# Order of VectorE's spectrum products in the middle stage of an FNet + H3 kernel

## The chip, the cores and the metric

The kernel runs on one core of a Trainium2 chip. The metric is the device time of one launch in microseconds, the median over several executions. Five engines work side by side, each on its own queue in order: TensorE (matmuls; PE in the profile, PEld is its loading of weights), VectorE (DVE), ScalarE (ACT), GpSimd (POOL) and SyncE (SP), whose queue here holds DMA issues.

## What is computed

Four layers follow each other, each added to its own input, on an input of 2048 rows by 576 channels; the first two are repeated with the same weights:

```python
x = x + A(layernorm(x))   # A: Real(DFT over rows of the DFT over channels), as matmuls with given matrices
x = x + B(layernorm(x))   # B: q * (long causal convolution of kv by ssm_k, + kv * ssm_D)
x = x + A(layernorm(x))
x = x + B(layernorm(x))

kv  = shift_convolution(k, 4 taps) * v
y_f = rfft(kv, 4096 points) * rfft(ssm_k, 4096 points)     # per channel, complex product
y   = irfft(y_f)[:2048] + kv * ssm_D
B   = q * y                                                # q is the normalised x
```

The branch B's factor y depends on k, v and the filter only, not on x. The kernel makes it once, while the first layer A runs, and uses it twice. What the change touches is the complex product of the two spectra.

## The kernel before, in words

All matmuls are split for accuracy: an operand is rounded to a high part and the rest is kept as a low part, and three products (high by high, high by low, low by high) are summed in PSUM. ScalarE makes the high part and VectorE the low part (`split`, lines 97 to 99; `act_split`, lines 516 to 518).

**The main stream.** Layer A is a loop over 128 steps (4 blocks of 512 output rows, the two DFT matrices, 16 row tiles). Each step has 12 matmuls of 128x512 into the four accumulators `s` and two into `rm`, all issued by `mm` on line 75. After a block's 32 steps its result goes through the channel DFT in `hidden` (lines 276 to 289): for each of four row tiles two halves of 27 matmuls of 128x288 (operands `u` and `w`), and VectorE adds each half to the residual on line 287.

**The branch stream.** Beside it the generator `branch` makes y. Its first part ends some 200 us into the run. Its middle stage, the one that matters here, works on 64 feeds (two halves of 288 channels, 32 groups of frequencies each). A feed is a 128x576 tile loaded from a DRAM scratch `td` (line 168, in `load_after`), the signal's spectrum lines in its first 288 columns and the filter's in the others. A visit to a feed does this:

- `mid_inverse` (line 541) for an earlier feed: three matmuls, one ScalarE copy `vo`, one store to `vd`.
- `mid_kernel` (line 520): three matmuls on the filter half into a bank `pk`, then three ScalarE copies on lines 522 to 524 (all recorded on line 512). The first takes all of `pk` into `kk[:,0]`. The second copies the upper 64 partitions of that to the upper half of `kk[:,1]`. The third overwrites the upper half of `kk[:,0]` by its lower half. So `p2 = kk[:,1]` holds the imaginary part in its upper half, and `p1 = kk[:,0]` the real part twice. `p2` is complete after the second copy, `p1` after the third.
- `mid_round` (line 536): the high and low part of the previous feed's product (`yf`): one ScalarE instruction and one 128x288 instruction on line 518.
- `mid_signal` (line 527): three matmuls on the signal half into a bank `px`, then four VectorE instructions, lines 530 to 533. Line 530 is the straight product over 128 partitions, `p1 = px*p1`. Line 531 makes the lower half of `p2` as minus the upper half of `px` times the upper half of `p2`. Line 532 overwrites the upper half of `p2` by the lower half of `px` times it, and so has to follow line 531. Line 533 adds `p2` to `p1`.
- `split_feed` (line 586): high and low part (`df`) of the feed two visits on, one ScalarE instruction and one 128x576 instruction on line 518. When it has read the raw feed, the raw buffer is free and `load_feed` (line 574) can load another.

From the 38th feed on, feeds of the last part are put between (`i2_products`, lines 550 to 560): four matmuls into two banks, two ScalarE copies, two VectorE additions on line 559, two stores to `yb`. About eight visits before that the raw feeds go down from three buffers to two (lines 616 to 622).

**Banks.** `bank` (line 83) gives the PSUM banks `bk` in turn, three of them, to `pv`, `pk` and `px` of the visits, to the products of the last part and to the halves of `hidden`. A bank can be written again once its last reader is done; for `px` that is the last of lines 530, 531 and 532 in VectorE's queue.

**What sets the order.** A hand-made budget (`STEP`, `PIECE`, `I2_COST` and the numbers that `branch` yields) decides between which matmuls of the main stream a visit is written. The order of the instructions in each engine's queue is made when the program is built and isn't strictly that of the source: where an instruction has to wait for one just before it, another that was written later may stand between the two. The trace shows it. `tc.issue_after` pins an instruction behind another on its engine; `act` uses it to keep the stage's ScalarE instructions in source order. Nothing pins the four VectorE instructions of `mid_signal`.

Of the kernel before, what the change touches and what calls it, by code (L numbers as in the profile page):

```python
# [13 lines left out]
OP = mybir.AluOpType  # L14
# [8 lines left out]
HD = D // 2  # L23
# [42 lines left out]
def fnet_h3_kernel(ctx: ExitStack, tc: tile.TileContext, x, c_mat, w_re, w_im, k_pad, v, shift_k,  # L66
                   ssm_k, ssm_d, f1c, i2c, midc, out):
    nc = tc.nc
# [280 lines left out]
    def branch():  # L349
# [150 lines left out]
        def mid_half(df, o):  # L500
            ps = bank()
            mm(ps[:, :HD], mc[:, 0, :], df[0][:, o:o + HD], True, False)
            mm(ps[:, :HD], mc[:, 0, :], df[1][:, o:o + HD], False, False)
            mm(ps[:, :HD], mc[:, 1, :], df[0][:, o:o + HD], False, True)
            return ps
# [21 lines left out]
        def mid_signal(df, kk):  # L527
            px = mid_half(df, 0)
            p1, p2 = kk[:, 0, :], kk[:, 1, :]
            nc.vector.tensor_tensor(p1, px[:, :HD], p1, OP.mult)  # L530
            nc.vector.scalar_tensor_tensor(p2[lo], px[hi, :HD], -1.0, p2[hi], op0=OP.mult, op1=OP.mult)  # L531
            nc.vector.tensor_tensor(p2[hi], px[lo, :HD], p2[hi], OP.mult)  # L532
            nc.vector.tensor_tensor(p1, p1, p2, OP.add)  # L533
            return p1

# [64 lines left out]
        for i, (kind, hf, q) in enumerate(feeds):  # L600
            df = halves.pop(i)
            if kind:
                i2_products(hf, q, fcs.pop(used), df)
                load_fc(used + ahead)
                used += 1
            else:
                if len(yfs) == MID_LAG:
                    mid_inverse(*yfs.pop(0))
                    yield 0.4
                kk = mid_kernel(df)  # L610
                if product is not None:
                    yfs.append((*product[:2], mid_round(product[2])))
                yield 1.6
                product = hf, q, mid_signal(df, kk)
# [540 lines left out]
```

## Time and profile before

| | |
|---|---|
| time, median of 3 (lowest to highest) | 1190.23 us (1188.69 to 1192.36) |
| the profiled execution | 1191.32 us, its span 1189.5 us |
| clock granted to TensorE in it | 0.998 of full speed |
| middle stage, first to last product of line 530 | 219.3 to 541.3 us |

The profile shows one execution. Its page gives each engine's busy share, the span in 40 slices, and groups of instructions with mean duration and the idle time before them. Of the trace, the waits are listed by who waited for whom, the timeline has the instructions in order of time, and the chain of waits follows back what ended last. Busy time of TensorE is the union of its matmuls, whose ends are modelled and overlap; its pace is seen better from the starts.

### The profile page before, as it was taken

How to read it: one execution, taken by the hardware profiler on the slowest of the kernel's cores; microseconds unless marked ns; L12 is line 12 of the kernel's file. 1: busy time of each engine (PE TensorE's matmuls, PEld its weight loads, DVE VectorE, ACT ScalarE, POOL GpSimd, SP SyncE). 2: the span in 40 equal slices, each digit the busy share in tenths (PEclk: the TensorE clock that was granted, in tenths of full speed). 3: DMA queues.
4: the chain of work that ended last, by engine and by line, in shares of the span. 5: the costliest groups of instructions: out<-in, count | busy, mean ns of one | idle time of the engine just before them, and what ended most of it. 6: DMA issues, size and time to landing. Idle time of an engine off the chain costs nothing.

```text
span 1189.5 us, 18071 instructions
## 1 busy us (share of the span) xinstructions
PE 1168.5 (98%) x6184; PEld 987.2 (83%) x6184; DVE 872.8 (73%) x1562; ACT 650.0 (55%) x1279; POOL 75.1 (6%) x116
## 2 busy tenths in 40 slices
PE   7999999999999999999999999999999999999997
PEld 5776767888888888888888898888888888889997
DVE  7899983688777778787767665865776776775764
ACT  7865555567766668766645666534444445450200
POOL 2210000000000000001101111000000000001111
PEclk9999999999999999999999999999999999999999
DMA  9869898545656656648966777772772776795621
GB/s 340 295 197 306 269 290 267 178 139 177 225 189 198 200 160 204 186 137 239 273 197 226 235 246 231 251 250 73 255 248 71 240 273 248 266 322 158 214 83 41
DMA packets 147454, 255.65 MB, mean 215 GB/s; under 512 B 16161, under 2 KB 56353, under 8 KB 147362
## 3 DMA queue, kind: packets, MB, share of 16 engines
q1 hardware_dynamic: 111890, 210.17, 54.9%
q10 hardware_dynamic: 28560, 37.91, 9.1%
q0 software_dynamic: 6912, 6.43, 2.4%
q8 instruction: 48, 0.79, 0.3%
q14 instruction: 44, 0.36, 0.1%
HBM read 187.80 MB, written 66.65 MB: 214 GB/s over the span
## 4 chain that ended last, share of the span: by engine, by line
PE 76%; ACT 2%; DVE 2%; DMA 2%; issue 1%; POOLq 0%; ACTq 0%; DVEq 0%
PE s L75 42%; PE bk L75 29%; PE rm L75 4%; ACT flts L512 1%; ACT mid L512 1%; DMA t<-ud 1%; DVE mid L518 0%; DMA yb<-flts 0%; DMA flts<-vd 0%; DMA flts<-in_c_mat 0%; DVE flts L532 0%; DVE flts L530 0%; ACT u L98 0%; DVE flts L531 0%; DVE flts L533 0%
## 5 line engine op out<-in xcount | busy, mean ns | idle before, releaser
L75 PE MATMUL s<-mats 128*128 128x512 f32 x2088 | 543.0, 395 | 1.6 <-ACT mats L195 0.8
L75 PEld LDWEIGHTS s<-mats 128*128 128x128 f32 x2088 | 381.0, 188 | 83.2 <-issue 10.6
L99 DVE TENSOR_TENSOR mats<-flts,mats 128x512 fp32r<-128x512 f32 x206 | 141.0, 688 | 50.8 <-ACT mats L98 48.4
L98 ACT ACTIVATE mats<-flts 128x512 fp32r<-128x512 f32 x206 | 128.3, 628 | 82.6 <-PE bk L75 31.2
L75 PE MATMUL bk<-mid 128*128 128x288 f32 x704 | 127.7, 302 | 1.6 <-DVE flts L287 0.8
L75 PEld LDWEIGHTS bk<-mid 128*128 128x128 f32 x704 | 108.0, 188 | 23.7 <-ACT flts L512 5.8
L512 ACT ACTIVATE flts<-bk 128x288 f32<-128x288 f32 (+1 forms) x192 | 76.3, 406 | 90.8 <-PE bk L75 75.9
L75 PE MATMUL bk<-w,u 128*128 128x288 f32 x864 | 121.3, 296 | 1.0 <-DVE w L241 0.4
L75 PEld LDWEIGHTS bk<-w,u 128*128 128x128 f32 x864 | 117.3, 188 | 5.5 <-DVE flts L532 1.7
L518 DVE TENSOR_TENSOR mid<-flts,mid 128x576 fp32r<-128x576 f32 (+1 forms) x149 | 93.4, 629 | 18.6 <-ACT mid L512 15.2
L75 PE MATMUL rm<-mats 128*128 128x512 f32 x304 | 94.6, 391 | 0.2 <-ACT flts L512 0.2
L512 ACT ACTIVATE mid<-flts 128x576 fp32r<-128x576 f32 (+1 forms) x148 | 80.3, 575 | 11.8 <-DVE flts L533 8.5
L287 DVE TENSOR_TENSOR flts<-flts,bk 128x288 f32<-128x288 f32 x48 | 21.8, 453 | 65.8 <-PE bk L75 65.7
L451 ACT ACTIVATE flts<-bf 128x384 f32<-128x384 f32 (+1 forms) x104 | 43.2, 463 | 46.0 <-PE bf L75 45.9
L75 PE MATMUL bk<-mats 128*128 128x288 f32 (+1 forms) x376 | 67.8, 317 | 0.0
L75 PEld LDWEIGHTS rm<-mats 128*128 128x128 f32 x304 | 56.9, 188 | 12.8 <-ACT flts L512 0.6
L75 PE MATMUL s<-t,mats 128*128 128x512 f32 x264 | 65.4, 390 | 0.6 <-DVE t L99 0.3
L184 POOL TENSOR_TENSOR flts<-flts 128x1 f32<-128x1 f32 x35 | 28.7, 821 | 522.4 <-DVE flts L183 522.3
L75 PE MATMUL bk<-mats,t 128*128 128x288 f32 (+1 forms) x368 | 59.3, 303 | 0.0
L512 ACT ACTIVATE flts<-flts 64x288 f32<-64x288 f32 x128 | 56.6, 443 | 4.7
L75 PEld LDWEIGHTS s<-t,mats 128*128 128x128 f32 x264 | 49.4, 188 | 11.7 <-DVE t L99 0.8
L75 PEld LDWEIGHTS bk<-mats 128*128 128x128 f32 x376 | 55.5, 188 | 3.4
(146 smaller groups left out, 1496.7 us busy)
## 6 DMA issues: line engine op xcount, KB each, us to landing
flts<-in_c_mat SPq DMA_DIRECT2D x148, 256.0 KB, 3.3
ph<-in_c_mat SPq DMA_DIRECT2D x54, 512.0 KB, 4.5
flts<-in_c_mat SPq DMA_DIRECT2D x30, 512.0 KB, 4.8
flts<-td SPq DMA_DIRECT2D x53, 288.0 KB, 2.9
td<-flts ACTq DMA_DIRECT2D x36, 384.0 KB, 4.6
vd<-flts ACTq DMA_DIRECT2D x64, 144.0 KB, 2.7
flts<-vd SPq DMA_DIRECT2D x32, 288.0 KB, 4.1
ud<-ph ACTq DMA_DIRECT2D x12, 512.0 KB, 6.3
```

The lines of the kernel that those rows point to most:

```text
L75: return nc.tensor.matmul(ps, lhsT, rhs, start=first, stop=last, skip_group_check=more).ins
L98: a = nc.scalar.activation(h, src, AF.Copy).ins
L99: return a, nc.vector.tensor_tensor(l, src, h.bitcast(F32), OP.subtract).ins
L184: pows.append(nc.gpsimd.tensor_tensor(rs, ve, mhalf, OP.pow).ins)
L287: added[:] = [nc.vector.tensor_tensor(r[:, cs], r[:, cs], ps[:, :HD], OP.add).ins]
L451: stored[:] = [nc.scalar.activation(so[:, i, :], ps[i], AF.Copy).ins]
L512: last_act.append(nc.scalar.activation(*args, **kw).ins)
L518: nc.vector.tensor_tensor(l, src, h.bitcast(F32), OP.subtract)
```

## The change

In `mid_signal` the straight product moves from the first to the third place. The four instructions, their operands and shapes are the same.

```diff
         def mid_signal(df, kk):
             px = mid_half(df, 0)
             p1, p2 = kk[:, 0, :], kk[:, 1, :]
-            nc.vector.tensor_tensor(p1, px[:, :HD], p1, OP.mult)
             nc.vector.scalar_tensor_tensor(p2[lo], px[hi, :HD], -1.0, p2[hi], op0=OP.mult, op1=OP.mult)
             nc.vector.tensor_tensor(p2[hi], px[lo, :HD], p2[hi], OP.mult)
+            nc.vector.tensor_tensor(p1, px[:, :HD], p1, OP.mult)
             nc.vector.tensor_tensor(p1, p1, p2, OP.add)
             return p1
```

## The prediction, made before the changed kernel was seen

> **What bounds the kernel now.** I read the page first, for the engine that is never idle, then the middle stage by stretches, then TensorE's pace there.
>
> ```profile
> PE 1168.5 (98%) x6184; PEld 987.2 (83%) x6184; DVE 872.8 (73%) x1562; ACT 650.0 (55%) x1279; POOL 75.1 (6%) x116
> ...
> 245.00:325.00 80.00, 79.72 (x431) 67.99 (x430) 68.15 (x134) 61.00 (x132) 0.00 (x0) 1.00 0.58 185
> ...
> 440.00:545.00 105.00, 104.39 (x549) 88.62 (x547) 87.00 (x166) 75.89 (x162) 3.69 (x7) 1.00 0.60 178
> ```
>
> The columns of the stretches are length, then busy time of PE, PEld, DVE, ACT and POOL. TensorE is busy for 79.72 of 80 us and 104.39 of 105 us. VectorE, which the change touches, has a sixth of those stretches free. But busy matmuls overlap in the record, so I check the pace by starts in the chain of waits:
>
> ```profile
> 307.41 1.38 PE s L75 x6
> 311.80 1.38 PE s L75 x6
> ...
> 650.82 2.72 PE s L75 x12
> 654.00 2.72 PE s L75 x12
> 666.69 3.55 PE bk L75 x27
> ```
>
> Near 650 us TensorE has only the main stream. Twelve matmuls of 128x512 take 2.72 us there, 0.227 us each, and 27 of 128x288 take 3.55 us near 667 us, 0.131 us each. A regular visit of the middle stage holds 14 of the first kind and 9 of the second: 14 x 0.227 + 9 x 0.131 = 4.36 us. The visits come 311.80 - 307.41 = 4.39 us apart. So in a regular visit TensorE runs at its own pace, and whatever VectorE's order does there is worth at most 0.03 us. Only irregular places can gain, and only a new wait can lose.
>
> [...]
>
> **The change part by part.** It adds and removes nothing. What is moved is seen in one regular visit on VectorE:
>
> ```profile
> 307.27 0.69 DVE L99 TENSOR_TENSOR mats<-flts,mats 128x512 fp32r<-128x512 f32 x1 [0.70 <-ACT mats L98]
> 307.88 0.45 DVE L530 TENSOR_TENSOR flts<-bk,flts 128x288 f32<-128x288 f32 x1
> 308.25 0.45 DVE L518 TENSOR_TENSOR mid<-flts,mid 128x288 fp32r<-128x288 f32 x1
> 308.73 0.46 DVE L531 SCALAR_TENSOR_TENSOR flts<-bk,flts 64x288 f32<-64x288 f32 x1
> 309.22 0.76 DVE L518 TENSOR_TENSOR mid<-flts,mid 128x576 fp32r<-128x576 f32 x1
> 310.01 0.45 DVE L532 TENSOR_TENSOR flts<-bk,flts 64x288 f32<-64x288 f32 x1
> 310.50 0.46 DVE L533 TENSOR_TENSOR flts<-flts 128x288 f32<-128x288 f32 x1
> 311.66 0.69 DVE L99 TENSOR_TENSOR mats<-flts,mats 128x512 fp32r<-128x512 f32 x1 [0.70 <-ACT mats L98]
> ...
> 310.01 0.32 SPq L168 DMA_DIRECT2D flts<-td  x1
> ...
> 311.24 0.55 PE L75 MATMUL bk<-mid 128*128 128x288 f32 x3
> ```
>
> Line 532 depends on line 531, and the queue has the feed's split (line 518, 128x576, 0.76 us) between the two, although the source has it behind line 533. After the change the straight product is the next instruction written behind the crossed pair, it depends on neither of them, and it is written ahead of the split. So I expect it to fill that gap: 531, 530, 532, split, 533 (or 531, 532, 530, split, 533 where the small split of line 518 stands behind 531). The sum of the durations is the same, and line 533 ends where it ended. Three things move.
>
> (a) **The bank of `px` comes free earlier**, by the split that no longer stands ahead of its last reader: 310.01 - 309.22 = 0.79 us in this visit. Here it buys nothing: line 532 ends at 310.46, and the next matmuls into that bank start at 311.24. It buys something where TensorE stands waiting for that reader:
>
> ```profile
> PEld bk L75 <- ACT flts L512: 6.7, 25, 0.7
> ...
> PEld bk L75 <- DVE flts L532: 4.5, 12, 0.8
> ...
> PE bk L75 <- DVE flts L532: 0.4, 1, 0.4
> ...
> 391.06 0.86 PE L75 MATMUL s<-mats 128*128 128x512 f32 x3
> 391.97 3.58 PEld L75 LDWEIGHTS bk<-w,u 128*128 128x128 f32 x27 [0.49 <-DVE flts L532]
> ...
> 403.84 0.62 PE L75 MATMUL rm<-mats 128*128 128x512 f32 x2
> 404.33 0.45 DVE L532 TENSOR_TENSOR flts<-bk,flts 64x288 f32<-64x288 f32 x1
> 404.83 2.29 PEld L75 LDWEIGHTS bk<-w,u 128*128 128x128 f32 x17 [0.80 <-DVE flts L532]
> ```
>
> Weight loads waited 4.5 us for line 532 in 12 places; matmuls alone show 0.4 us. The loss of pace lies between. At 391.97 us three matmuls from 391.06 at 0.227 us each would have ended at 391.74, so 0.23 of the 0.49 us is lost; at 404.83 two from 403.84 would have ended at 404.29, so 0.54 of 0.80 us. Together 0.77 of 1.29, that is 60%, and 0.6 x 4.5 = 2.7 us. The longest wait is 0.80 us and the bank comes 0.79 us earlier, so I take all 2.7 us as gained. Bounds: 4.5 us gained at most, and 0 if the matmuls are also queued earlier and wait as long as before.
>
> (b) **The first product can start before the third copy of line 524**, since line 531 needs only the second:
>
> ```profile
> DVE flts L530 <- ACT flts L512: 15.2, 14, 2.2
> ...
> L512 ACT ACTIVATE flts<-flts 64x288 f32<-64x288 f32 x128 | 56.6, 443 | 4.7
> ```
>
> VectorE stood idle 14 times ahead of line 530 for ScalarE. One copy is 0.443 us, so 14 x 0.443 = 6.2 us of VectorE's idle time may go. No release to TensorE but that of (a) hangs on it, which (a) already counts in full: I take 0, with 2.7 us more as the far end of a gain, a second sum like that of (a).
>
> (c) **The feed's split comes one product later**, 0.45 to 0.49 us. Behind it on VectorE stand line 533 and the main stream's splits, which move by nothing, as the sum is equal. Behind it on SP stands the load of another feed: in the visit above it is issued at 310.01, right when the split is done, and now is issued at about 310.5. Behind that load in SP's queue stand the loads of the DFT matrix.
>
> ```profile
> SPq L168 <- DVE mid L518: 122.6, 57, 5.2
> SPq L168 <- DVE mats L99: 51.6, 39, 4.8
> ...
> 391.36 0.68 ACT L512 ACTIVATE mid<-flts 128x576 fp32r<-128x576 f32 x1 [0.62 <-DMA flts<-td]
> ...
> PEld bk L75 <- DVE mid L518: 0.7, 3, 0.3
> ```
>
> SP waits for that split in 57 places, so the lateness reaches the DMA each time. Whether it reaches TensorE is the question: the loads of the matrix wait for line 99 anyway (39 times), one feed's ScalarE half stood 0.62 us waiting for its load, and weight loads waited for the split for only 0.7 us in all. I take 0, bounded by a gain of 0 (nothing gets earlier) and the loss of the second rival.
>
> GpSimd's queue waits for nothing that moves in the steady part: its filter loads follow TensorE and the last part's buffers. Line 533 feeds `mid_round` one visit on; as its end doesn't move, neither does that.
>
> **Sum.** The profiled execution took 1191.32 us, with a span of 1189.5 us; it lies 1.1 us above the median of 1190.23 and inside the three runs. From it 2.7 us go: 1188.6 us, and from the median **1187.5 us**, -0.2%. That is less than 0.3% (3.6 us), about what a measurement of this kernel can tell from no change.
>
> **The rivals.**
>
> *Nothing reaches TensorE.* The matmuls behind the earlier bank are queued earlier too, or the planner keeps today's order with the straight product merely elsewhere. For it: the regular visit has 0.78 us to spare (310.46 to 311.24) and doesn't use it. Against: the waits at 391.97 and 404.83 us stand directly behind line 532. Time: 1190.2 us, within a microsecond.
>
> *Slower: the loop of the raw feeds.* In the later part of the stage there are two raw buffers. A buffer goes from split to SP's load, to ScalarE's half, to the split again, and the split is now a product later in each visit.
>
> ```profile
> L530 DVE TENSOR_TENSOR flts<-bk,flts x31: 447/454/459, 371.9 to 541.3; 128x288 f32<-128x288 f32 x31
> ```
>
> There are 31 visits from 371.9 us on. Passed on whole, each costs a product, 0.46 us: 31 x 0.46 = 14.3 us, 1204.5 us. It decides from 8 visits on (8 x 0.46 = 3.7 us). For it: the wait of 0.62 us at 391.36 shows a load that is only just in time. Against: only one such wait is in the list, and 0.7 us for the split on TensorE. If half of them pass it on, 7.1 us less the 2.7 gained: 1194.6 us.
>
> *Faster: ScalarE's evictions come earlier as well.* Weight loads also wait 6.7 us for ScalarE's copies out of the banks, in 25 places, 0.6 x 6.7 = 4.0 us of pace, and ScalarE itself waits for VectorE:
>
> ```profile
> ACT mid L512 <- DVE flts L533: 8.5, 9, 1.9
> ...
> ACT flts L512 <- DVE flts L531: 4.6, 10, 0.5
> ```
>
> If (b) shortens these waits, the copies behind them on ScalarE come earlier and the 4.0 us go too: 1190.2 - 2.7 - 4.0 = 1183.5 us. Against: the evictions wait mostly for TensorE. [...]
>
> **How the numbers follow.** Forecast 0.42, of which 0.06 ends beyond 3.6 us (towards all 4.5 us of (a)); nothing reaches TensorE 0.18, of which 0.02 ends beyond 3.6 us on the slow side, through other places of the queues; slower by the feeds 0.22; faster with ScalarE 0.18. So faster 0.06 + 0.18 = 0.24, slower 0.22 + 0.02 = 0.24, within 0.3% 0.36 + 0.16 = 0.52. The range reaches from 1183.5 (the faster case) to 1196.0 (the feed loop with a few visits more than half: 18 x 0.46 - 2.7 = 5.6 us), leaving out half of each outer case, some 0.2. The forecast's own range is 1185.7 to 1190.2.
>
> **What would show it.** Right: on VectorE line 530 stands between 531 and 533 ahead of the 128x576 split; the list of waits has less than 1 us of weight loads behind line 532 or 530; the visits stay 4.39 us apart. Wrong in (c): weight loads wait several us for line 518, ScalarE waits for DMAs from `td` or `vd`, and visits after 372 us are further apart. Wrong in (a): the waits for line 532 turn up behind line 530 with the same sum. If VectorE's order is otherwise than I expect, (a) and (c) both fall.

## The result, and the profile after

| | before | after |
|---|---|---|
| median of 12 runs each (lowest to highest) | 1190.38 us (1188.69 to 1195.69) | 1187.27 us (1185.74 to 1190.31) |
| the profiled execution, its span | 1191.32, 1189.5 us | 1186.46, 1184.5 us |

The ratio is 0.9972, with a 95% interval of 0.9964 to 0.9980: 3.3 us less, 2.4 to 4.3. Forecast were 2.7 us and 1187.5 us.

In the changed kernel line 530 is the first crossed product, 531 the second, 532 the straight one, now the last reader of `px`, and 533 the sum. Its page, the line of TensorE:

```profile
PE 1165.9 (98%) x6184; PEld 988.1 (83%) x6184; DVE 868.8 (73%) x1562; ACT 650.6 (55%) x1279; POOL 75.0 (6%) x116
```

The work is the same, 6184 matmuls and 1562 VectorE instructions. TensorE's busy time is 2.6 us shorter and the span 5.0 us. The difference is sought in the middle stage. First the regular visit of the prediction, on VectorE, with SP's load of a feed and the chain of waits (start, length; idle time before it in brackets):

```profile
304.46 0.69 DVE L99 TENSOR_TENSOR mats<-flts,mats 128x512 fp32r<-128x512 f32 x1 [0.70 <-ACT mats L98]
305.18 0.46 DVE L530 SCALAR_TENSOR_TENSOR flts<-bk,flts 64x288 f32<-64x288 f32 x1
305.68 0.46 DVE L518 TENSOR_TENSOR mid<-flts,mid 128x288 fp32r<-128x288 f32 x1
306.17 0.45 DVE L531 TENSOR_TENSOR flts<-bk,flts 64x288 f32<-64x288 f32 x1
306.63 0.46 DVE L532 TENSOR_TENSOR flts<-bk,flts 128x288 f32<-128x288 f32 x1
307.01 0.75 DVE L518 TENSOR_TENSOR mid<-flts,mid 128x576 fp32r<-128x576 f32 x1
307.67 0.45 DVE L533 TENSOR_TENSOR flts<-flts 128x288 f32<-128x288 f32 x1
...
307.78 0.32 SPq L168 DMA_DIRECT2D flts<-td  x1
...
304.60 1.38 PE s L75 x6
308.99 1.38 PE s L75 x6
```

The small split of line 518 stands between the crossed products, the straight product behind both, and the feed's split (128x576) behind that. The last reader ends 307.09 - 305.18 = 1.91 us after the first product starts; before it was 310.46 - 307.88 = 2.58 us. The feed's split starts 1.83 us after the first product instead of 1.34, so 0.49 us later, and SP's load 2.60 us after it instead of 2.13. The visits are still 4.39 us apart.

What has changed for TensorE shows in the waits of the stage, 215 to 545 us (who waited for whom, us in all, times, longest):

```profile
DVE flts L530 <- ACT flts L512: 10.6, 9, 2.0
...
ACT mid L512 <- DMA flts<-td: 2.2, 4, 0.7
...
PEld bk L75 <- DVE flts L532: 1.4, 4, 0.6
...
PEld bk L75 <- DVE mid L518: 0.8, 3, 0.3
...
PE bk L75 <- DVE flts L532: 0.2, 1, 0.2
```

Weight loads wait 1.4 us for the last reader, in 4 places, where it was 4.5 us in 12. They wait 0.8 us for line 518 (0.7 before). VectorE stands idle for ScalarE 10.6 us ahead of its first product instead of 15.2. The second of the two waits shown in the prediction is gone (timeline of the changed kernel, at the same matmuls):

```profile
399.21 0.46 DVE L532 TENSOR_TENSOR flts<-bk,flts 128x288 f32<-128x288 f32 x1
399.58 0.75 DVE L518 TENSOR_TENSOR mid<-flts,mid 128x576 fp32r<-128x576 f32 x1
...
400.77 0.62 PE L75 MATMUL rm<-mats 128*128 128x512 f32 x2
401.01 3.74 PEld L75 LDWEIGHTS bk<-w,u 128*128 128x128 f32 x27
401.24 3.75 PE L75 MATMUL bk<-w,u 128*128 128x288 f32 x27
```

The two matmuls into `rm` start at 400.77, at 0.227 us each they end at 401.22, and the next matmul starts at 401.24. Before, 0.54 us were lost here.

Where the time went can be counted over all matmuls. Taking from each distance between two starts TensorE's own pace (0.227 or 0.131 us) and summing what is left from 212 to 560 us gives 16.2 us lost before and 13.0 us after. At the matmuls whose load waits for the last reader of `px` it is 3.1 us before (12 places) and 0.9 us after (4). This counts the held matmul and the one behind it, which mostly starts another 0.11 us late, as at 404.83 and 405.07 us before; the held ones alone make 1.8 and 0.5 us. The same matmuls of the main stream start 1.2 us earlier already ahead of the stage (209.1 and 207.9 us), where both kernels have the same code, and 4.8 us earlier behind it (at 590 us). So in this pair of profiled executions 3.6 us lie between these two points, and 1.2 us are a difference between executions. Of the 3.6 us some 2.2 are seen directly behind the last reader; the rest is spread over other places.

### The profile page after: what moved, and what is told of

It is laid out like the page before. It is cut to its first block, busy times and chain, and to the rows that moved or that the text cites. A ratio compares the mean times of both kernels' runs of the same rounds, so it can differ in the third digit from the quotient of the medians.

```text
span 1184.5 us, 18056 instructions
## 1 busy us (share of the span) xinstructions
PE 1165.9 (98%) x6184; PEld 988.1 (83%) x6184; DVE 868.8 (73%) x1562; ACT 650.6 (55%) x1279; POOL 75.0 (6%) x116
## 4 chain that ended last, share of the span: by engine, by line
PE 77%; ACT 2%; DMA 1%; DVE 1%; issue 0%; ACTq 0%; POOLq 0%; DVEq 0%
PE s L75 43%; PE bk L75 30%; PE rm L75 4%; ACT flts L512 1%; ACT mid L512 1%; DMA t<-ud 1%; DMA flts<-in_c_mat 0%; ACT mats L98 0%; DVE mid L518 0%; DVE flts L532 0%; DVE flts L531 0%; DVE t L99 0%; ACT u L98 0%; POOLq L1151 0%; ACTq L548 0%
## 5 line engine op out<-in xcount | busy, mean ns | idle before, releaser
L75 PEld LDWEIGHTS s<-mats 128*128 128x128 f32 x2088 | 381.0, 188 | 82.2 <-issue 10.6
```

What stands on the lines that cost most here:

```text
L75: return nc.tensor.matmul(ps, lhsT, rhs, start=first, stop=last, skip_group_check=more).ins
```

## The experiments

Four causes were possible: the bank of `px` is free earlier (part (a)); the first product starts before the third copy (b); the split comes later (c, a cost); and a fourth that the prediction hadn't priced. When VectorE's order changes, the order of TensorE's queue is made anew too: 477 of the 6184 matmuls stand at another place, all between the 1045th and the 2889th. The runs with "old tensor" in their name pin the matmuls to the order that they have in the kernel before, by an order without a wait (`NoSync`) between each matmul and the next (`mm` appends every matmul to `traced`; the pieces are cut out of the source):

```python
traced = []
...
queue = [traced[a + i] for a, n in ORDER_OF_MATMULS for i in range(n)]
for one, two_ in zip(queue, queue[1:]):
    tc.add_manual_dep(two_, one.name, mybir.DependencyInfo(
        mybir.DependencyClass.NoSync, mybir.DependencyReason.DATA), reason="order of matmuls")
```

In the pinned kernels the lines stand further down: `mm` on 101 or 102, ScalarE on 539 or 540, the split on 545 or 546, the products from 557 to 563. The table has all runs. "Gained" is (1 - ratio) x 1191 us with the interval worked out in the same way. "Reader" and "split" are weight loads' waits for the last reader of `px` and for line 518 (in before, after, e1, e7 and e8 all of these places but one are behind a 128x576 split, in e10 all), "first" is VectorE's wait for ScalarE ahead of its first product, all in us between 215 and 545 us.

| kernel | split in between | early start | TensorE's queue | ratio (95%) | gained, us | reader | split | first |
|---|---|---|---|---|---|---|---|---|
| before | 54 | no | old | 1 | 0 | 4.5 | 0.7 | 15.2 |
| after | 18 | yes | new | 0.9972 (0.9964 to 0.9980) | 3.3 (2.4 to 4.3) | 1.4 | 0.8 | 10.6 |
| e1 | 0 | no | made anew | 0.9994 (0.9985 to 1.0003) | 0.7 (-0.4 to 1.8) | 1.2 | 1.8 | 16.9 |
| e7 | 0 | no | old | 0.9988 (0.9979 to 0.9996) | 1.4 (0.5 to 2.5) | 0.6 | 2.6 | 13.8 |
| e3 | 48 | yes | made anew | 0.9984 (0.9975 to 0.9993) | 1.9 (0.8 to 3.0) | 1.4 | 0.6 | 11.4 |
| e9 | 48 | yes | old | 0.9994 (0.9986 to 1.0003) | 0.7 (-0.4 to 1.7) | 2.4 | 1.1 | 9.7 |
| e4 | 20 | no | made anew | 0.9989 (0.9980 to 0.9998) | 1.3 (0.2 to 2.4) | 2.1 | 1.0 | 17.5 |
| e8 | 21 | no | old | 0.9999 (0.9990 to 1.0007) | 0.1 (-0.8 to 1.2) | 1.6 | 1.6 | 16.2 |
| e5 | 19 | yes | old | 0.9978 (0.9969 to 0.9987) | 2.6 (1.5 to 3.7) | 0.9 | 0.5 | 10.2 |
| e6 | 52 | no | of after | 1.0033 (1.0021 to 1.0044) | -3.9 (-5.2 to -2.5) | 3.6 | 0.5 | 15.5 |
| e10 | 0 | yes | old | 0.9968 (0.9956 to 0.9980) | 3.8 (2.4 to 5.2) | none | 0.7 | 10.2 |
| e12 | 0 | yes | made anew | 0.9958 (0.9944 to 0.9972) | 5.0 (3.3 to 6.7) | 0.6 | 0.9 | 9.8 |
| e2 | 0 | yes | made anew | 0.9992 (0.9983 to 1.0001) | 1.0 (-0.1 to 2.0) | 2.0 | 0.9 | 10.2 |
| e11 | 0 | yes | old | 0.9988 (0.9979 to 0.9997) | 1.4 (0.4 to 2.5) | 0.5 | 0.5 | 12.3 |

"Split in between" counts, of 64 visits, those in which a 128x576 split stands between the first product and the last reader of `px`; where it doesn't, the bank is early. From the first product's start to the last reader's end it takes 2.43 us on the mean before, 2.04 after, 1.86 in e1, 2.41 in e9 and 1.84 in e12.

A second measure can be read from each trace: the time between the starts of the 1041st and the 2901st matmul, between which all moved ones lie. Against before it is shorter by 3.4 us in after, 3.3 in e12, 3.1 in e10, 2.6 in e5, 2.3 in e3, 1.5 in e1, 1.4 in e4, 1.3 in e9, 0.7 in e11, 0.3 in e2 and e8 and 0.2 in e7, and longer by 2.5 us in e6. Each is one execution, but the order is nearly that of the times.

### The bank alone: e1_source_order_split_behind

The source order of before, and the feed's split pinned behind the last reader of `px` (`behind` puts `tc.issue_after` around what it encloses; `kind` is 0 for a feed of this stage):

```diff
-            nc.vector.tensor_tensor(p2[hi], px[lo, :HD], p2[hi], OP.mult)
+            last_px[:] = [nc.vector.tensor_tensor(p2[hi], px[lo, :HD], p2[hi], OP.mult).ins]
...
-            split_feed(i + 2)
+            with behind(*(last_px if not kind else [])):
+                split_feed(i + 2)
```

> The source order of before (straight product first), with one thing pinned: the 128x576 split of line 518 stands behind the last product that reads the bank of px, in all 64 visits (before: ahead of it in most). The first product still waits for the third copy. Theory A, the bank that comes free earlier: 2.5 to 4.5 us under before, as fast as the changed kernel or a little faster, and weight loads wait under 1.5 us for the last product. Theory B, the earlier start of the first product: within 1 us of before. Theory C, another draw of queue order without a mechanism: anywhere within 4 us of before, and the waits for the last product don't go along with the time.

0.9994 (0.9985 to 1.0003). The waits of e1 in the stage:

```profile
ACT mid L512 <- DMA flts<-vd: 3.3, 3, 1.3
ACT mid L512 <- DMA flts<-td: 2.9, 4, 1.1
PEld bk L75 <- DVE mid L518: 1.8, 6, 0.4
...
PEld bk L75 <- DVE flts L532: 1.2, 5, 0.4
```

The wait for the last reader went from 4.5 to 1.2 us, as part (a) says, but the time hardly followed: weight loads now wait 1.8 us for the split, and ScalarE 6.2 us for transfers of feeds (0.6 before). Part (a) alone, with (b) and (c) taken as 0, doesn't carry the result.

### The straight product in the middle: e2_straight_in_the_middle

```diff
-            nc.vector.tensor_tensor(p1, px[:, :HD], p1, OP.mult)
             nc.vector.scalar_tensor_tensor(p2[lo], px[hi, :HD], -1.0, p2[hi], op0=OP.mult, op1=OP.mult)
+            nc.vector.tensor_tensor(p1, px[:, :HD], p1, OP.mult)
             nc.vector.tensor_tensor(p2[hi], px[lo, :HD], p2[hi], OP.mult)
```

> Straight product in the second place, between the crossed ones; nothing pinned. In VectorE's queue the 128x576 split then stands behind the last reader of px in all visits but 2, in the changed kernel in 44 of 64. Theory A: at least the gain of the changed kernel, 3 to 4.5 us under before. Theory B: the first product still starts without the third copy, so the same gain as the changed kernel, 3 us. Theory C: no better guess than within 4 us of before.

0.9992 (0.9983 to 1.0001), although it has the early bank and the early start. Between the crossed products stands now the straight one, often with the small split of line 518, and in no visit the feed's split. I come back to it at e11.

### The split kept ahead: e3_split_ahead

The changed order, with the straight product pinned behind the feed's split, so that the bank comes free as late as before; `split_feed` is called from `mid_signal`, directly behind `mid_half`, and returns its VectorE instruction:

```diff
-        def mid_signal(df, kk):
+        def mid_signal(df, kk, i):
             px = mid_half(df, 0)
+            low = split_feed(i)
...
-            nc.vector.tensor_tensor(p1, px[:, :HD], p1, OP.mult)
+            with behind(*low):
+                nc.vector.tensor_tensor(p1, px[:, :HD], p1, OP.mult)
```

> The changed order, with the feed's split written ahead of the products and the straight product (the last reader of px) pinned behind it: the bank comes free as late as in before or later, the start of the first product stays early. Theory A: the gain is lost, at before or up to 3 us slower, and weight loads wait 4 us or more behind line of the straight product. Theory B: the gain stays, 2 to 4 us under before. Theory C: within 4 us of before either way.

0.9984 (0.9975 to 0.9993): the early start without the early bank, and a gain of 1.9 us, though with a queue of TensorE of its own.

### The start taken away: e4_first_waits_for_third_copy

The changed order, whose first crossed product waits for the third copy as the straight product did:

```diff
+            copy3[:] = [last_act[-1]]
...
-            nc.vector.scalar_tensor_tensor(p2[lo], px[hi, :HD], -1.0, p2[hi], op0=OP.mult, op1=OP.mult)
+            first = nc.vector.scalar_tensor_tensor(p2[lo], px[hi, :HD], -1.0, p2[hi], op0=OP.mult, op1=OP.mult).ins
+            tc.add_manual_dep(first, copy3[0].name, mybir.DependencyInfo(
+                mybir.DependencyClass.Sync, mybir.DependencyReason.DATA), reason="third copy")
```

> The changed order, with one wait more: the first crossed product waits for the third ScalarE copy, as the straight product did in before. The order of the queue is nearly that of the changed kernel (split behind the last reader of px in 42 visits instead of 44). Theory A: as the changed kernel, 2 to 4 us under before. Theory B: the gain is lost, within 1 us of before. Theory C: within 4 us of before either way.

0.9989 (0.9980 to 0.9998). It lies between what was expected for the bank and for the start. These four kernels each got a queue of TensorE of their own, and their gains, 0.7 to 1.9 us, don't order the causes. So the next runs hold that queue still.

### VectorE's order or TensorE's: e5_new_vector_old_tensor and e6_old_vector_new_tensor

e5 is the changed source with the matmuls in the order of before. e6 is the source of before with the matmuls in the order of after.

> The changed source, with all matmuls pinned in TensorE's queue to the order that they have in before. The first four runs took theory A down as it stood (source order with the split behind: 1 us, not 3), so it is now: D, the gain lies in the order of TensorE's queue, which the build makes anew when VectorE's instructions are turned round. D: within 1.2 us of before. A', VectorE's own order (earlier bank and earlier start) makes the gain, TensorE's order only follows: 2 to 4 us under before.

> The other corner: the source of before, with all matmuls pinned to the order that they have in the changed kernel. D, the order of TensorE's queue makes the gain: 2 to 4 us under before. A', VectorE's own order makes it: at before, or up to 2 us slower, since matmuls then stand earlier than the bank that the old order frees later, and weight loads wait 5 us or more for the last product. If both corners give about half, the two belong together.

e5 is at 0.9978 (0.9969 to 0.9987), e6 at 1.0033 (1.0021 to 1.0044). The waits of e5, then of e6:

```profile
DVE flts L558 <- ACT flts L540: 10.2, 10, 2.0
...
PEld bk L102 <- DVE flts L560: 0.9, 3, 0.6
...
PEld bk L102 <- DVE mid L546: 0.5, 2, 0.3
```

```profile
PEld bk L101 <- DVE flts L559: 3.6, 7, 1.2
PEld s L101 <- DVE u L126: 3.5, 3, 2.9
...
PE bk L101 <- DVE flts L559: 1.5, 4, 0.7
```

With the old queue of TensorE the change keeps 2.6 of its 3.3 us, and the waits for reader and split fall as in after. With the new queue and the old order of VectorE, TensorE comes to the bank too early, waits 1.2 us for the reader in one place, and the kernel loses 3.9 us, more than the up to 2 us expected. The largest wait of it is of another kind, at the end of a block of layer A (timeline of e6):

```profile
441.05 0.76 DVE L545 TENSOR_TENSOR mid<-flts,mid 128x576 fp32r<-128x576 f32 x1
...
441.84 0.45 DVE L559 TENSOR_TENSOR flts<-bk,flts 64x288 f32<-64x288 f32 x1
442.32 0.69 DVE L126 TENSOR_TENSOR u<-s,u 128x512 fp32r<-128x512 f32 x1
...
443.06 1.23 PEld L101 LDWEIGHTS s<-mats 128*128 128x128 f32 x6 [2.88 <-DVE u L126]
443.06 1.66 PE L101 MATMUL s<-mats 128*128 128x512 f32 x6 [2.45 <-DVE u L126]
```

The block's accumulator `s` has to be emptied by ScalarE and by VectorE's split on line 126, and that split stands behind a whole visit in VectorE's queue: TensorE waits 2.45 us once. So the gain comes with VectorE's order, not with the queue that TensorE got; that queue loses time under the old order of VectorE. The other pairs with the same source say the same (e1 and e7, e2 and e11, e3 and e9, e4 and e8, e12 and e10): holding TensorE's queue moves none by more than 1.2 us, and the intervals overlap in each.

### The parts one by one with TensorE's queue held: e7 to e10

e7 is e1, e8 is e4, e9 is e3, each with the matmuls in the order of before. e10 is the changed source with the split pinned behind the straight product in every visit, with the same pin of the matmuls:

```diff
-            nc.vector.tensor_tensor(p1, px[:, :HD], p1, OP.mult)
+            last_px[:] = [nc.vector.tensor_tensor(p1, px[:, :HD], p1, OP.mult).ins]
             nc.vector.tensor_tensor(p1, p1, p2, OP.add)
...
-            split_feed(i + 2)
+            with behind(*(last_px if not kind else [])):
+                split_feed(i + 2)
```

> Once more the source order of before with the split of line 518 pinned behind the last product that reads px, now with TensorE's queue pinned to the order of before. The bank comes free earlier, the first product starts no earlier, and no matmul moves. Theory Aa, the earlier bank makes the gain: 2 to 3 us under before. Theory Ab, the earlier start of the first product makes it: within 1 us of before.

> The changed order with the first product waiting for the third copy, TensorE's queue pinned to the order of before. The bank comes free earlier (42 visits have the split behind its last reader), the start is as late as in before. Aa: 1.5 to 3 us under before. Ab: within 1 us of before.

> The changed order with the split written ahead of the products and the straight product pinned behind it, TensorE's queue pinned to the order of before. Early start, late bank. Aa: the gain is lost, at before or up to 3 us slower, with weight loads waiting 4 us or more for the straight product. Ab: 2 to 3 us under before.

> The changed order with the split pinned behind the straight product in all 64 visits (44 in the changed kernel), TensorE's queue pinned to the order of before: early start and early bank everywhere. Aa and Ab: at least as fast as the changed kernel, 3 to 4 us under before. If the later split costs something (the slower rival of the prediction): 1 to 2 us under before, with weight loads waiting more for line 518's split than in before.

The bank alone (e7) gains 1.4 us, the start alone (e9) 0.7 us, both in all visits (e10) 3.8 us. Neither single cause came out as expected: e8 speaks for the start and e9 against it. e5 and e8 have nearly the same order on VectorE (19 and 21 splits in between) and differ in the early start: 2.6 against 0.1 us, so the start is worth 2.5 us there, with half-widths of 1.1 and 1.0 us. e10 and e9 differ in the early bank: 3.1 us, with 1.4 and 1.0. So each is worth 2.5 to 3 us beside the other. That each is worth less alone is suggested, not shown. In the pinned kernels 1.4 and 0.7 make 2.1 us against 3.8, with half-widths of 1.0, 1.0 and 1.4. In the unpinned ones e1 and e3 make 2.6 us against 5.0 in e12 by the times, but 3.8 against 3.3 by the second measure. The waits of e7 show what stands against its early bank:

```profile
ACT mid L540 <- DMA flts<-td: 4.3, 4, 2.3
PEld bk L102 <- DVE mid L546: 2.6, 7, 0.6
...
PEld bk L102 <- DVE flts L560: 0.6, 2, 0.4
```

And the longest of them in its timeline:

```profile
415.97 0.62 PE L102 MATMUL rm<-mats 128*128 128x512 f32 x2
416.74 0.68 ACT L540 ACTIVATE mid<-flts 128x576 fp32r<-128x576 f32 x1 [2.26 <-DMA flts<-td]
417.44 0.41 ACT L540 ACTIVATE flts<-bk 128x288 f32<-128x288 f32 x1
417.45 0.76 DVE L546 TENSOR_TENSOR mid<-flts,mid 128x576 fp32r<-128x576 f32 x1 [0.61 <-ACT mid L540]
417.90 3.59 PEld L102 LDWEIGHTS bk<-w,u 128*128 128x128 f32 x27 [1.74 <-ACT flts L540]
417.90 3.83 PE L102 MATMUL bk<-w,u 128*128 128x288 f32 x27 [1.31 <-ACT flts L540]
```

This is read from top to bottom: ScalarE's half of a feed waits 2.26 us for the feed's load; behind it on ScalarE stands a copy that frees a bank; TensorE waits 1.31 us for that bank. It is the loop of the raw feeds, the prediction's second rival, in one place, and the largest loss of TensorE in e7's stage; e1, with the same order of source, has none as long. Against the 3.9 us that the waits for the reader lose (4.5 to 0.6 us) stand 1.9 us more for the split. In e10, with the early start and the split behind the last reader too, both waits are smaller (waits of e10):

```profile
DVE flts L558 <- ACT flts L540: 10.2, 10, 2.0
...
ACT mid L540 <- DMA flts<-td: 1.2, 2, 0.7
...
PEld bk L102 <- DVE mid L546: 0.7, 2, 0.5
```

### The middle order once more, and the split pinned in all visits: e11_middle_old_tensor and e12_all_behind_free_tensor

e11 is e2 with the matmuls in the order of before. e12 is e10 without that pin.

> The straight product in the second place, as in the second run (1 us under before, although start and bank are early there), now with TensorE's queue pinned to the order of before. Theory AB, early start and early bank together make the gain, and the build's new order of the matmuls took 2 to 3 us of it back in the second run: 3 to 4 us under before. If the place of the straight product itself is what costs (its wait for the third copy stands ahead of a crossed product): again about 1 us under before.

> The kernel of the tenth run (changed order, split pinned behind the straight product in all visits) without the pinned matmuls: the form that one would keep. Theory AB with a harmless order of the matmuls: 3 to 4.5 us under before, at or a little under the changed kernel. If the build's order of the matmuls is a draw that can take 2 to 3 us, as in the second run: 1 to 2 us under before.

e12 is at 0.9958 (0.9944 to 0.9972), 5.0 us, the lowest time of all, from 5 runs. It is 1186.02 us, against 1187.27 of the change; the two intervals overlap between 0.9964 and 0.9972, and by the second measure it gains 3.3 us where the change gains 3.4, so I don't call it faster than the change. Against the kernel before the whole interval is a gain. Its waits for these two have little left:

```profile
PEld bk L75 <- DVE mid L518: 0.9, 4, 0.2
...
PEld bk L75 <- DVE flts L532: 0.6, 2, 0.3
```

e11 is at 0.9988 (0.9979 to 0.9997). The 3 to 4 us expected of early bank and early start didn't come; the time is near the other expectation, that the place of the straight product costs. It has the early bank and start, and both sorts of waits are small (0.5 and 0.5 us); what it loses, it loses elsewhere (its timeline at the end of a block):

```profile
259.27 0.98 PE L102 MATMUL s<-mats 128*128 128x512 f32 x3 [0.67 <-DVE u L127]
...
262.82 0.63 ACT L126 ACTIVATE u<-flts 64x512 fp32r<-64x512 f32 x1 [2.53 <-DVE flts L301]
...
264.67 0.67 PE L102 MATMUL bk<-mid 128*128 128x288 f32 x3 [1.45 <-ACT flts L540]
```

As in e6, VectorE's work at the end of a block (the split of `u`, the sum on line 301) stands behind a visit in its queue: the sum starts at 262.12 us there and at 259.33 in e10. Some 2 us are lost there (0.67 and 1.45 us of idle time on TensorE). TensorE's queue is the same in both; what places the work there on VectorE, the products' order or the chance of how its queue was made, wasn't told apart.

## Why the prediction was right, and where not

**The time and the class.** 1187.5 us was forecast, 1187.27 measured, 0.28% below before, on the border between the two classes that the prediction separated at 0.3%.

**The bound.** Right: the regular visits stay 4.39 us apart, and only irregular places gained.

**The order on VectorE.** Half right. The straight product stands ahead of the feed's split as expected, but not in the gap between the crossed products: the small split fills that, and the straight product is last. In 18 of 64 visits (54 before) the feed's split itself is in the gap, and the bank comes as late as before. The cause of the gap was read rightly, what fills it wasn't: the prediction took the next instruction in the source, while in the trace one that was ready earlier took the place. On the mean of all visits the last reader ends 2.43 - 2.04 = 0.39 us sooner after the first product's start, and not 0.79.

**(a), the bank, 2.7 us.** Its signs came: the wait of weight loads for the last reader fell by 3.1 us, to 1.4 and not below 1 us, and TensorE's loss behind it by 2.2 us of the 3.1 that were there. The 60% were read at the two longest waits, where only the held matmul was counted; held matmuls alone make 1.8 us over the 12 places, and with the matmul behind each 3.1, so 2.7 us was near by two errors against each other. And the step counted the bank as if it paid in full by itself. Without the early start it paid 1.4 us (e7) or 0.7 (e1).

**(b), the early start, taken as 0.** This step failed. The prediction said that no release to TensorE hangs on it but that of (a), "which (a) already counts in full". The runs give it some 2.5 us where the bank is early: e8 0.1 us and e5 2.6, e7 1.4 and e10 3.8. VectorE's idle time ahead of the first product fell by 4.6 of the 6.2 us worked out, so the size of the head start was about right. What it does was missed. The waits of e10 against e7 suggest that what follows on VectorE in such a visit comes earlier too, the split and with it the feeds' loads; no run moves these alone.

**(c), the later split, taken as 0.** Its waits came, and its price isn't measured. The split is 0.49 us later in the regular visit, counted from the first product, as worked out; counted from line 99's split it is 0.60 us. Where no early start offsets it (e1, e7), weight loads wait 1.8 to 2.6 us for the split instead of 0.7, and ScalarE 4.9 to 6.2 us for feeds' loads instead of 0.6. In the changed kernel these waits are 0.8 and 2.2 us; the early start of up to 0.44 us, one copy, would explain it. So (b) was a gain and (c), as far as the waits tell, a cost: that 2.7 us came out near the measured 3.3 with both at 0 is in part luck.

**The rivals.** That nothing reaches TensorE fell. The feeds' loop is real in single places but was outweighed. The faster rival, ScalarE's evictions, didn't come (waits of the changed kernel):

```profile
PEld bk L75 <- ACT flts L512: 5.9, 20, 0.6
...
ACT flts L512 <- ACT flts L512: 5.0, 11, 0.5
```

Weight loads still wait 5.9 us for ScalarE's copies (6.7 before). ScalarE's wait for the first crossed product, 4.6 us in 10 places, is gone, but in 11 places a copy now waits for the copy ahead of it, 5.0 us in all (0.4 us in one place before).

**What the prediction didn't have:** TensorE's queue is made anew. It wasn't the cause here, but it can cost as much as the effect: under the old order of VectorE the new queue loses 3.9 us (e6). VectorE's own queue matters as much: 7.3 us lie between after and e6 (0.9972 and 1.0033 of before), which have the same queue of TensorE, and kernels with bank and start both early lie 2.4 (e10 and e11, TensorE's queue the same) and 4.0 us (e12 and e2) apart.

**Open:** why e2 and e11, with bank and start both early, gain only 1.0 and 1.4 us. Losses of theirs at block ends are seen (in e2 TensorE stands 1.04 us at 440.22), what places VectorE's work there isn't settled. e3 and e9 differ by 1.2 us, and their intervals overlap. The pinned kernels hold TensorE's queue alone; VectorE's and ScalarE's queues are still made anew in each, so that e8 isn't exactly e5 without the start. As such a queue can be worth 2.4 us (e10 and e11), how the gain divides between bank and start stays open; that it comes with VectorE's order doesn't.

## What to carry to other kernels

When an order of independent instructions is chosen, put the last reader of a shared bank as early as its inputs allow, and look in the trace for unrelated work that was placed between; then pin that work behind it (e12, as fast as the change or a little faster). Price what is displaced as well: here the earlier release gained 0.7 to 1.4 us while the split came later, and 2.6 to 5.0 where the same move let the whole group start earlier, unless the straight product stood in the middle (1.0 and 1.4). And before a few tenths of a per cent are put down to a change on one engine, pin the queue of the engine that sets the end, since that queue may have been made anew; here that ruled it out as the cause.

## What the runs showed of the hardware

VectorE's busy time fell from 872.8 to 868.8 us with the same 1562 instructions. In the visits shown, some instructions start before the one ahead of them has ended, and some don't. Line 518's 128x576 split starts 0.38 us after line 532, which lasts 0.46 us, and line 533 starts 0.66 us after that split of 0.75 us. Before, line 532 started 0.79 us after the same split (0.76 us), and line 533 0.49 us after line 532 (0.45 us). In the two visits shown the crossed products, which read or write half the partitions, and what follows them start only when the one ahead has ended (0.46 to 0.50 us from start to start behind one of 0.45 or 0.46 us), while a full 128-partition instruction behind another starts before that (0.37 and 0.38 us behind one of 0.45 or 0.46). What decides between the two isn't shown, and the number of partitions alone doesn't: at 391.95 us of the kernel before, an addition of line 559 on 64 partitions lasts 0.46 us, and line 533 on 128 starts 0.38 us after it. The visit shown gets no shorter by the overlap: from line 99's start to the sum's end it takes 308.12 - 304.46 = 3.66 us now and 310.96 - 307.27 = 3.69 before; the first product now starts 0.72 us after line 99's split, which lasts 0.69 us, and started 0.61 us after it before.
